# Local-global attention with a gated MLP: TensorE blocks of two attention units, scores four units ahead, residual halves added early, and the order drawn from 40 plans

## The chip, the cores and the metric

The kernel runs on one core of one Trainium2 chip. The metric is device microseconds (us) of one execution. The kernel before takes 427.39 us, the median of three runs (426.9 to 428.18).

## What is computed

Two stages follow each other for each of 4 batches. The first is attention with 8 heads, 768 positions and head size 64, in which a query sees the first 8 positions and the last 96, with a bias linear in the distance. The second is a gated MLP over the 768 x 512 result.

```python
scores = scale * q @ k^T + bias            # kept: key < n_global, or 0 <= rel < n_local
a = softmax(where(keep, scores, -1e9)); x = a @ v          # heads side by side: 768 x 512
h = gelu(x @ w_in); u, v = halves of h
v_n = (v - mean) / sqrt(var + 1e-6) * g_ln
v_s = w_sg @ v_n + b_sg                    # mixes the 768 positions
out = x + (u * v_s) @ w_out
```

## The kernel before, in words

**Attention** is cut into 48 units: a batch (4), two heads (4 pairs), and 256 query positions (3). Within a batch the four pairs of the first 256 positions come first. A unit has three pieces of TensorE work, all in 64x64 quarters of the array: the scores (`score`, matmuls on L714, into two PSUM banks), for the first 16 units a transposition by a diagonal matrix (`turn_quarters`, L845, two banks), and p.v (`weigh`, L873, two banks named av). p.v has a first part and a second, `again`, which adds into the same columns and so waits until the first part is done; between the two, TensorE has the scores of another unit. After the scores, VectorE adds the bias and takes the minimum (L745), ScalarE takes the exponential (L750), and for units from the 17th p is divided by its sum on GpSimd, ScalarE or VectorE (L767), transposed in 32x32 blocks by VectorE (L809) and sent through DRAM by DMA (far, then pt). The av banks are read out as two halves, x and the rest that x lost in rounding, by L929 and L933 from the 25th unit on (L947, L959, L961, L965 before).

**The MLP** runs in full 128x128 matmuls, three for each product (high x high, high x low, low x high: L413, L414, L415, called `terms`). Its tiles are v (512 columns; gelu and norm), u (384; gelu), mix (w_sg times the normed v, then times u) and out. An out tile adds both halves of x to the bank (L524 for the first, L526 for the second) and is sent off on SyncE's queue (L529).

**What sets the order.** The program is written down as a list of operations, each with the engines that may do it and a cost on each. `Plan.due` gives each operation a time at which it is needed. `Plan.order` then walks through time: on each free engine it starts the operation that is due first among those whose inputs are there and whose buffers have a place. TensorE's list is kept nearly in the written order. Numbers steer it: CALM and PATIENCE (an operation that is not urgent may wait for a cheaper engine), PRICE (a surcharge on VectorE), EARLY (how long ahead a load may be issued), SPARE (how many further PSUM banks must be free before an MLP tile opens one), TO_QUARTERS and FROM_QUARTERS (what TensorE loses when it goes from whole-array matmuls to quarters and back). What comes out is a fixed order on each engine's queue. Buffers have the places that PLACES gives: 8 PSUM banks, 2 each of v and pt, 4 of p, 3 of qk, 1 of tt, 4 of t.

**The written order** comes from `step(n)`: load v for n + 1 and qk for n + 4, first part of p.v of unit n, transposition of unit n + 1, scores of unit n + 3 (AHEAD is 3), second part of p.v of unit n, softmax of n + 3. `phase` puts MLP products between the steps. So TensorE goes into quarters once for each unit, for one block of p.v and scores, and back. In the last phase o[1][0..2], three out tiles, take turns product by product, and the fourth follows.

**At the start** VectorE makes the table of distances (L600, L601 and L655 to L667) from GpSimd's iota rows and from n_global and n_local, which come by DMA (tile ni). The bias of each head is made from it (L685, L687). TensorE is given matmuls on zeros (L364) where it would idle up to 29 us.

## Time and profile before

| | us |
|---|---|
| median of 3 runs | 427.39 |
| the profiled execution | 425.15 |
| its span, first to last instruction | 423.3 |
| TensorE (PE) busy | 407.6, 96% |
| VectorE (DVE) busy | 304.6, 72% |
| ScalarE (ACT) busy | 235.1, 56% |
| GpSimd (POOL) busy | 202.0, 48% |

A profile row gives the line of the kernel, the engine, the operation, the tile written and those read, the shapes and the count. In a timeline, the first two numbers are the start and the length in us. Matmuls overlap: the time that one really costs is from its start to the next one's start, not its length. An fp32 matmul in quarters shows as two records, so 4 matmuls in an order are 8 in a timeline.

### The profile page before, as it was taken

The numbers are of one execution on the slowest core, as the hardware profiler recorded it, in microseconds if no ns is written. First come the engines' busy times: TensorE is split into PE (matmuls) and PEld (weight loads), VectorE is DVE, ScalarE is ACT, GpSimd is POOL, SyncE is SP. The second block draws the span as 40 slices with busy tenths as digits, with TensorE's granted clock in tenths as the row PEclk, the third lists the DMA queues.
The fourth block names the chain that finished last, engine by engine and source line by source line (L and its number), as shares of the span: only waits on it lengthen the run. The fifth ranks groups of instructions, "written<-read, shape, count | busy, mean of one in ns | idle before, by whom it ended". The sixth has DMA issues, their size and how long they took to land.

```text
span 423.3 us, 13841 instructions
## 1 busy us (share of the span) xinstructions
PE 407.6 (96%) x5328; PEld 370.6 (88%) x5328; DVE 304.6 (72%) x990; ACT 235.1 (56%) x787; POOL 202.0 (48%) x312
## 2 busy tenths in 40 slices
PE   8989999899999999999999999999999999999994
PEld 8877777799888888999999888999999878999994
DVE  6887899999966879866566888966566866743343
ACT  5999989866657575654246566554245434311220
POOL 2223446668577586452545466452545443323211
PEclk9999999999999999999999999999999999999998
DMA  7656493347888776553877766463886631001002
GB/s 250 217 183 187 153 291 111 125 131 215 241 258 275 197 246 168 133 153 106 242 234 219 213 197 177 125 158 108 244 248 170 168 108 38 2 0 57 19 2 81
DMA packets 50041, 68.22 MB, mean 161 GB/s; under 512 B 5808, under 2 KB 33968, under 8 KB 49968
## 3 DMA queue, kind: packets, MB, share of 16 engines
q1 hardware_dynamic: 49968, 67.26, 54.2%
q8 instruction: 44, 0.72, 0.7%
q14 instruction: 29, 0.24, 0.2%
HBM read 48.89 MB, written 18.35 MB: 159 GB/s over the span
## 4 chain that ended last, share of the span: by engine, by line
PE 76%; DVE 9%; ACT 7%; DMA 3%; issue 2%; POOL 1%; SPq 0%; POOLq 0%; DVEq 0%
PE mm_ps L413 21%; PE mm_ps L415 19%; PE mm_ps L414 19%; PE av L873 8%; PE s_ps L714 6%; ACT p L750 3%; PE tps L845 2%; DMA far<-tt 2%; DMA stage<-in_w_sg_t_dram 1%; DVE stage L570 1%; DVE stage L572 1%; DMA ni<-in_n_gl_dram 1%; DVE p L745 1%; DVE o L524 1%; DVE tt L809 1%
## 5 line engine op out<-in xcount | busy, mean ns | idle before, releaser
L750 ACT ACTIVATE p<-p,pst 128x192 f32<-128x192 f32 x192 | 84.1, 443 | 7.4 <-DVE pst L745 6.9
L767 POOL TENSOR_SCALAR p<-p,pst 128x192 f32<-128x192 f32 (+1 forms) x128 | 56.0, 454 | 21.9 <-DVE pst L759 15.4
L413 PE MATMUL mm_ps<-wsg,z 128*128 128x384 f32 x192 | 65.1, 339 | 0.4 <-ACT pt L853 0.4
L415 PE MATMUL mm_ps<-wsg,z 128*128 128x384 f32 x192 | 64.3, 335 | 0.0
L745 DVE CUSTOM_DVE_ANT_0 p<-s_ps,bias 128x192 f32<-128x192 f32 x192 | 57.3, 340 | 9.7 <-PE s_ps L714 9.4
L414 PE MATMUL mm_ps<-wsg,z 128*128 128x384 f32 x192 | 64.3, 335 | 0.0
L873 PE MATMUL av<-pt,v 64*64 64x128 f32 (+1 forms) x1408 | 54.6, 254 | 2.6 <-DMA far<-tt 1.7
L873 PEld LDWEIGHTS av<-pt,v 64*64 64x64 f32 x1408 | 38.8, 133 | 16.8 <-issue 7.0
L526 POOL TENSOR_TENSOR o<-o,x 128x384 f32<-128x384 f32 x30 | 30.4, 1014 | 44.5 <-DVE o L524 31.9
L413 PE MATMUL mm_ps<-x,win 128*128 128x384 f32 x128 | 44.3, 346 | 0.8 <-ACT pt L853 0.8
L714 PE MATMUL s_ps<-qk 64*64 64x128 f32 (+1 forms) x1408 | 42.5, 247 | 1.7 <-issue 1.0
L413 PE MATMUL mm_ps<-gt,wout 128*128 128x384 f32 x128 | 43.0, 336 | 0.0
L415 PE MATMUL mm_ps<-gt,wout 128*128 128x384 f32 x128 | 43.0, 336 | 0.0
L415 PE MATMUL mm_ps<-x,win 128*128 128x384 f32 x128 | 42.9, 335 | 0.0
L414 PE MATMUL mm_ps<-x,win 128*128 128x384 f32 x128 | 42.8, 335 | 0.0
L414 PE MATMUL mm_ps<-gt,wout 128*128 128x384 f32 x128 | 42.8, 335 | 0.0
L506 POOL TENSOR_TENSOR y<-y,u 128x384 f32<-128x384 f32 x20 | 20.3, 1014 | 43.0 <-DVE y L503 28.2
L413 PE MATMUL mm_ps<-win,x 128*128 128x512 f32 x96 | 40.4, 421 | 0.0
L445 ACT CAST gt<-y 128x384 fp32r<-128x384 f32 x29 | 14.9, 512 | 45.9 <-DVE y L506 23.5
L714 PEld LDWEIGHTS s_ps<-qk 64*64 64x64 f32 x1408 | 37.5, 134 | 2.7 <-issue 1.3
L413 PEld LDWEIGHTS mm_ps<-wsg,z 128*128 128x128 f32 x192 | 36.0, 188 | 2.1 <-issue 1.4
L415 PE MATMUL mm_ps<-win,x 128*128 128x512 f32 x96 | 37.6, 392 | 0.0
(105 smaller groups left out, 937.7 us busy)
## 6 DMA issues: line engine op xcount, KB each, us to landing
qk<-in_qk_in_dram SPq DMA_DIRECT2D x32, 352.0 KB, 3.9
far<-tt SPq DMA_DIRECT2D x96, 96.0 KB, 2.6
pt<-far SPq DMA_DIRECT2D x24, 384.0 KB, 3.5
v<-in_v_in_dram SPq DMA_DIRECT2D x32, 256.0 KB, 3.3
out_dram<-o SPq DMA_DIRECT2D x32, 192.0 KB, 2.8
qk<-in_qk_in_dram SPq DMA_DIRECT2D x16, 288.0 KB, 3.6
v<-in_v_in_dram SPq DMA_DIRECT2D x16, 192.0 KB, 3.6
far<-tt SPq DMA_DIRECT2D x32, 80.0 KB, 1.9
```

Of the source, the lines that this page charges most:

```text
L413: mm(ps.ap, ah, bh, start=(i == 0), stop=False)
L414: mm(ps.ap, ah, bl, start=False, stop=False)
L415: mm(ps.ap, al, bh, start=False, stop=(i == n - 1))
L445: put(out[:, 0, :], src.ap)
L506: by_u = lambda eng: eng.tensor_tensor(y.ap, y.ap, gt.ap, ALU.mult)
L526: lo = lambda eng: eng.tensor_tensor(o.ap, o.ap, xm[:, 1, :].bitcast(F32), ALU.add)
L714: nc.tensor.matmul(s_ps[h][e * HQ:(e + 1) * HQ, i * W + c0:i * W + c0 + n], qk[rows, qc:qc + HQ], qk[rows, QW + k0:QW + k0 + n], start=Tru ...
L745: nc.vector.tensor_tensor_reduce(out=p[:, g, 0:nk], in0=s_ps[h][:, i * W:i * W + nk], in1=bias[:, 2 * j + h, w0:w0 + nk], op0=ALU.add, op1 ...
L750: op([on_act(nk, 0.225) + (lambda p=p, g=g, nk=nk, i=i: nc.scalar.activation(p[:, g, 0:nk], p[:, g, 0:nk], AF.Exp, bias=st[:, 0, i, g:g + ...
L767: op([on_pool_ts(nk, -0.10) + (partial(scaled, lambda o, a, c: nc.gpsimd.tensor_scalar(o, a, c, 1.0, ALU.mult, ALU.mult)),), on_act(nk, 0. ...
L845: nc.tensor.matmul(tps[r][g * HQ:(g + 1) * HQ, a * HQ:(a + 1) * HQ], pc[rows, c:c + HQ], diag[rows, 2 * i + c // W], start=True, stop=True)
L873: nc.tensor.matmul(to, v[rows, vc:vc + D], of, stop=True, skip_group_check=True, **kw)
```

## The change

From the 25th unit on (PAIRS = 24) `step` takes two units: it writes down the scores of one unit, the first parts of p.v of both, the scores of the next unit, then both second parts. The pair shares two av banks (columns 0 to 127 and 128 to 255). Scores are then written four units ahead of the pair instead of three. For out tiles of the last half of the last batch, the two halves of x are added to each other in advance (L548 of the new kernel, after the tile's first product), and one add of the bank follows. The distances take fewer VectorE operations, and those that don't need n_global and n_local come first. FROM_QUARTERS goes from 0.11 to 0.21, the spare banks from 2 to 0 once the scores of 27 units are written down. `order` draws CALM, EARLY, PRICE and a small shift of each due time from a seed; 40 seeds are planned and the plan that ends first by the planner's own clock is emitted.

```diff
-CALM, PATIENCE = 5.0, 2.0
-PRICE = 0.3
-EARLY = 12.0
+PLANS = 40
+CALM, PATIENCE = (3.0, 12.0), 2.0
+PRICE = (0.1, 0.4)
+EARLY = (9.0, 17.0)
+APART = 0.2
-SPARE = 2
+SPARE, SPARE_LATE = 2, 0
+PAIRS = 24
-TO_QUARTERS, FROM_QUARTERS = 0.095, 0.11
+TO_QUARTERS, FROM_QUARTERS = 0.095, 0.21
...
-        for o in self.order(start):
+        self.due()
+        ends = [self.order(start, seed)[1] for seed in range(PLANS)]
+        for o in self.order(start, ends.index(min(ends)))[0]:
...
+        whole = self.temp("o", CH) if last else None
+
+        def ahead(first):
+            xm = x[m][c]
+            both = lambda eng: eng.tensor_tensor(whole.ap, xm[:, 0, :].bitcast(F32),
+                                                 xm[:, 1, :].bitcast(F32), ALU.add)
+            op([on_dve_sb(CH) + (lambda: both(nc.vector),),
+                on_pool(CH) + (lambda: both(nc.gpsimd),)], [xm], [whole], [first])
...
-    future(rel, tmp)
...
+    def distances():
+        future(rel, tmp)
...
+        vec.tensor_scalar(key, key, ng, FAR, ALU.is_ge, ALU.mult)
+        vec.scalar_tensor_tensor(tmp, rel, nl, key, ALU.is_ge, ALU.mult)
+        vec.scalar_tensor_tensor(dist[:, 0:W], rel[:, 0:W], nl, tmp[:, 0:W], ALU.min, ALU.max)
+        vec.scalar_tensor_tensor(dist[:, 2 * W:], rel[:, W:], nl, tmp[:, W:], ALU.min, ALU.max)
...
-    dist_b.since = 6.3
+    dist_b.since = 5.6
...
         def put():
-            shared(0)
-            for e in range(2):
...
+            for m in range(len(ns)):
+                shared(m, 0)
+                for e in range(2):
...
-    def step(n):
-        m = n + AHEAD
...
+    def group(n):
+        return list(range(n, n + 1 + (n >= PAIRS)))
+
+    def step(ns):
+        nonlocal scored
+        end = ns[-1] + 1
+        nexts = [n for n in group(end) if 0 <= n < len(units)]
+        more = list(range(scored, min(end + AHEAD + (end >= PAIRS), len(units))))
+        scored += len(more)
...
+        for n in more[:-1]:
+            score(n, [])
+        if end > 0:
+            first, rest = weigh(ns)
+        for n in nexts:
+            turn(n)
+        for n in more[-1:]:
...
+            between.append(score(n, [first] if first else []))
```

**The blocks.** On TensorE, around the last phase of the third batch, a block of one unit before (p.v of the 36th unit, scores of the 39th):

```order
L415 MATMUL mm_ps<-gt,wout 128x384
L873 MATMUL av<-pt,v 64x128 x4
L873 MATMUL av<-pt,v 64x64 x8
L714 MATMUL s_ps<-qk 64x128 x8
L714 MATMUL s_ps<-qk 64x64 x4
L873 MATMUL av<-pt,v 64x128 x4
L413 MATMUL mm_ps<-win,x 128x512
```

After, the block with p.v of the 33rd and 34th unit (L761 are the scores, L922 is p.v):

```order
L435 MATMUL mm_ps<-wsg,z 128x384
L761 MATMUL s_ps<-qk 64x128 x8
L761 MATMUL s_ps<-qk 64x64 x4
L922 MATMUL av<-pt,v 64x128 x4
L922 MATMUL av<-pt,v 64x64 x8
L922 MATMUL av<-pt,v 64x128 x4
L922 MATMUL av<-pt,v 64x64 x8
L761 MATMUL s_ps<-qk 64x128 x8
L761 MATMUL s_ps<-qk 64x64 x4
L922 MATMUL av<-pt,v 64x128 x8
```

Two units' work now stands in one stretch of quarters. Counted over the whole order, from the first block of the 25th unit to the end there were 27 such stretches and are now 16: nine blocks of a pair in one piece, three pairs that the planner tore into two, and one block with the scores of the 29th unit alone. Up to there it was 23 stretches and is 23.

**The end.** On VectorE, the last rows of the program, before (gt and y belong to the last mix tile):

```order
L503 SCALAR_TENSOR_TENSOR y<-mm_ps,g,bsg 128x384
L506 TENSOR_TENSOR y<-y,u 128x384
L449 TENSOR_TENSOR gt<-y,gt 128x384
L524 TENSOR_TENSOR o<-mm_ps,x 128x384
L526 TENSOR_TENSOR o<-o,x 128x384
L524 TENSOR_TENSOR o<-mm_ps,x 128x384 x2
L526 TENSOR_TENSOR o<-o,x 128x384
L524 TENSOR_TENSOR o<-mm_ps,x 128x384
```

After, the sums of the halves of x (L548) stand between the last mix tile's operations and one add for each tile is left (L556); GpSimd's queue, which held the other two L526, holds none at the end:

```order
L525 SCALAR_TENSOR_TENSOR y<-mm_ps,g,bsg 128x384
L548 TENSOR_TENSOR o<-x 128x384
L528 TENSOR_TENSOR y<-y,u 128x384
L548 TENSOR_TENSOR o<-x 128x384 x2
L471 TENSOR_TENSOR gt<-y,gt 128x384
L556 TENSOR_TENSOR o<-mm_ps,o 128x384 x3
L548 TENSOR_TENSOR o<-x 128x384
L556 TENSOR_TENSOR o<-mm_ps,o 128x384
```

The four L548 are new on VectorE, and no add of x follows the last product but one.

**The start.** VectorE's rows for the distances after the change (L633 and L634 are the two of `future`, L703 is the first that needs ni; before, the two stood behind it, as L600 and L601):

```order
L633 TENSOR_SCALAR setup<-setup 128x320
L634 TENSOR_TENSOR setup<-setup 128x320
L703 SCALAR_TENSOR_TENSOR nv<-ni 128x2
L704 SCALAR_TENSOR_TENSOR nv<-nv,ni 128x2
L707 TENSOR_SCALAR setup<-setup,nv 128x320
L708 SCALAR_TENSOR_TENSOR setup<-setup,nv 128x320
L709 SCALAR_TENSOR_TENSOR dist<-setup,nv 128x192
L710 SCALAR_TENSOR_TENSOR dist<-setup,nv 128x128
```

Two rows moved ahead of the wait for ni, and two fewer follow it. Elsewhere operations went from one engine to another: of the halves of z, y and gt, 28 went from GpSimd to VectorE, and of L767, 22 went from GpSimd to ScalarE and 3 to VectorE.

## The prediction

> **What bounds the kernel now.** I read the page's first part, then busy time in windows, then TensorE's timeline at two blocks, then its waits, and last the two ends.

> ```profile
> PE 407.6 (96%) x5328; PEld 370.6 (88%) x5328; DVE 304.6 (72%) x990; ACT 235.1 (56%) x787; POOL 202.0 (48%) x312
> ```

> TensorE (PE) leads by far, but a busy PE isn't yet a PE that does work. Where it is short of work the windows say:

> ```profile
> core 0: us, PE busy (x) PEld busy (x) DVE busy (x) ACT busy (x) POOL busy (x), PEclk, DMA share, GB/s
> 20.00:31.00 11.00, 9.50 (x347) 8.23 (x347) 9.83 (x30) 10.37 (x40) 3.88 (x4) 1.00 0.64 207
> 31.00:40.00 9.00, 8.01 (x241) 6.47 (x238) 5.85 (x30) 8.20 (x32) 2.60 (x6) 1.00 0.65 186
> 60.00:90.00 30.00, 27.25 (x383) 24.14 (x383) 27.55 (x89) 26.02 (x87) 18.38 (x25) 1.00 0.40 121
> 120.00:130.00 10.00, 9.05 (x107) 8.39 (x106) 5.73 (x20) 4.74 (x20) 6.39 (x10) 1.00 0.96 307
> 130.00:153.00 23.00, 21.71 (x320) 18.88 (x319) 17.44 (x56) 13.29 (x49) 15.43 (x28) 1.00 0.81 233
> 165.00:260.00 95.00, 95.00 (x1126) 86.90 (x1122) 69.16 (x234) 51.04 (x172) 49.23 (x82) 1.00 0.66 185
> ```

> The column that matters is PE busy beside the length. Up to 31 us ScalarE (ACT) sets the pace, busy 10.37 of 11.00. Between 31 and 153 PE lacks 0.99, 2.75, 0.95 and 1.29 us in four windows, 6.0 together. From 165, where the 25th unit's block begins, it lacks nothing, at full clock (PEclk 1.00): there the time is what PE's instructions cost, and only fewer or cheaper ones shorten it. What a block of quarters costs beside its matmuls shows in the timeline, first where a block is whole, then where the same p.v is in two pieces:

> ```profile
> 207.50 0.34 PE L415 MATMUL mm_ps<-gt,wout 128*128 128x384 f32 x1
> 207.77 0.68 PE L873 MATMUL av<-pt,v 64*64 64x128 f32 x24
> 208.27 0.85 PE L714 MATMUL s_ps<-qk 64*64 64x128 f32 x32
> 208.94 0.40 PE L873 MATMUL av<-pt,v 64*64 64x128 f32 x8
> 209.27 0.44 PE L413 MATMUL mm_ps<-x,win 128*128 128x384 f32 x1
> 209.55 0.34 PE L414 MATMUL mm_ps<-x,win 128*128 128x384 f32 x1
> ```

> ```profile
> 334.30 0.33 PE L414 MATMUL mm_ps<-gt,wout 128*128 128x384 f32 x1
> 334.47 0.34 PE L415 MATMUL mm_ps<-gt,wout 128*128 128x384 f32 x1
> 334.74 0.68 PE L873 MATMUL av<-pt,v 64*64 64x128 f32 x24
> 335.35 0.50 PE L413 MATMUL mm_ps<-win,x 128*128 128x512 f32 x1
> 335.69 0.39 PE L414 MATMUL mm_ps<-win,x 128*128 128x512 f32 x1
> 335.92 0.40 PE L415 MATMUL mm_ps<-win,x 128*128 128x512 f32 x1
> 336.24 0.45 PE L873 MATMUL av<-pt,v 64*64 64x128 f32 x8
> 336.62 0.50 PE L413 MATMUL mm_ps<-win,x 128*128 128x512 f32 x1
> 336.96 0.39 PE L414 MATMUL mm_ps<-win,x 128*128 128x512 f32 x1
> ```

> From start to start a 384-column matmul takes 0.17 us (334.30 to 334.47), a 512-column one 0.23 (335.69 to 335.92). The whole block stretches the two steps from 207.50 to 209.55 to 2.05 us; less 2 x 0.17 it costs 1.71. Its scores run from 208.27 to 208.94, 0.67, so p.v with one entry and one exit costs 1.04. In two pieces the same p.v costs 1.22 - 0.17 - 0.23 = 0.82 (334.47 to 335.69) and 1.04 - 2 x 0.23 = 0.58 (335.92 to 336.96), 1.40 together. One more entry and exit therefore costs **0.36 us**.

> **The change part by part. Fewer blocks.** By the order, from the 25th unit on TensorE enters quarters 16 times instead of 27, with the same matmuls. 11 x 0.36 = 4.0 us, all of it in the stretch where PE lacks nothing, so it comes off the end if no wait takes its place. [...] The rows with p.v whole and in pieces measure the thing itself, so the sum goes by 0.36.

> **The end.** The last gt and the product that reads it, and then the last chain of work:

> ```profile
> 410.91 0.56 DVE L449 TENSOR_TENSOR gt<-y,gt 128x384 fp32r<-128x384 f32 x1 [0.58 <-ACT gt L445]
> 413.53 0.33 PE L413 MATMUL mm_ps<-gt,wout 128*128 128x384 f32 x1
> 417.00 0.34 PE L415 MATMUL mm_ps<-gt,wout 128*128 128x384 f32 x1
> 417.38 0.56 DVE L524 TENSOR_TENSOR o<-mm_ps,x 128x384 f32<-128x384 f32 x1
> 418.07 0.99 POOL L526 TENSOR_TENSOR o<-o,x 128x384 f32<-128x384 f32 x1 [1.03 <-DVE o L524]
> 415.50 3.92 SPq L529 DMA_DIRECT2D out_dram<-o  x4
> ```

> After, the store can go when L524's successor is done: 417.94 instead of 419.06, 1.1 us less; SyncE's queue, which issues the four stores up to 419.42, waits for nothing else then. The four sums of x halves stand on VectorE (DVE) instead, at about 0.56 us each by L524. Three stand in the last mix tile's chain: one delays its gt by 0.56, the other two fall into the 0.58 that DVE waited there and delay it by 2 x 0.56 - 0.58. gt was ready at 411.47 and is read from 413.53 on, so these 1.1 us stay hidden; without that cover they would cost 1.1, the whole gain. The fourth sum fits in DVE's wait for the last product. I take 1.1, with 0 as the other end.

> **The start.** The distances on VectorE, from the first row that needs ni to the first bias:

> ```profile
> 3.80 0.16 DVE L655 SCALAR_TENSOR_TENSOR nv<-ni 128x2 f32<-128x2 int32 x1 [2.81 <-DMA ni<-in_n_gl_dram]
> 4.48 0.32 DVE L601 TENSOR_TENSOR setup<-setup 128x320 bf16<-128x320 bf16 x1
> 4.84 0.30 DVE L660 TENSOR_SCALAR setup<-setup,nv 128x320 bf16<-128x320 bf16 x1
> 5.18 0.33 DVE L662 TENSOR_TENSOR setup<-setup 128x320 bf16<-128x320 bf16 x1
> 5.42 0.30 DVE L663 TENSOR_SCALAR setup<-setup,nv 128x320 bf16<-128x320 bf16 x1
> 6.37 0.29 DVE L685 TENSOR_SCALAR bias<-dist 128x512 bf16<-128x512 bf16 x1
> ```

> L600 and L601 move into the wait of 2.81 us, and L660 and L662 become one operation, as do L663 and the two L664, L665. From start to start L601 costs 0.36 us, L660 0.34 and L662 0.24; with L663 and L600 taken at 0.24 like the last, 1.2 us leave the chain. No row shows a fused operation; each of the three may take up to 0.12 more than what it replaces (0.36 against 0.24), so 0.8 to 1.2 are left, and I take 0.8. ACT, which paces the first 31 us, starts by as much sooner; its order there is nearly the same. Ends: 1.2, and 0 if a load becomes the later one.

> **The drawn plan.** In the first 24 units the order enters quarters 23 times as before, and MLP products lie about where they lay. So the 6.0 us that PE lacks between 31 and 153 can shrink or grow, and no row says which. I take 0, with 4.0 less (two thirds of it gone) and 5.0 more (nearly as much again) as ends.

> **The moved operations.** 28 operations of 0.56 to 0.69 us go from GpSimd (POOL) to DVE, about 17 us on an engine that is busy 69.16 of 95 us from 165 to 260. PE covers it; if DVE were late, a bank would come free late, which is the second rival. The guard of p.v (L899) now holds its engine's queue until both first parts are done, by the rows above some 0.5 us longer, once for two units; what stands behind it there is late by that, beside PE's next products.

> Sum: -4.0 - 1.1 - 0.8 = **-5.9 us**. The profiled execution has 425.15 (span 423.3 and 1.85 around it) and would come to 419.25. The median of before lies 2.24 above that execution, so I forecast 427.39 - 5.9 = **421.5 us**.

> **The rivals.** *Transfers of a pair come late (slower).* v and pt have two places each, and a pair holds all four until its block ends. Both units' transfers must then land before the next block:

> ```profile
> pt<-far SPq DMA_DIRECT2D x24, 384.0 KB, 3.5
> v<-in_v_in_dram SPq DMA_DIRECT2D x32, 256.0 KB, 3.3
> PE av L873 <- DMA far<-tt: 1.7, 2, 1.0
> ```

> That is 1280 KB, 4.2 us at the 307 GB/s of the busiest window, and a landing of 3.5: 7.7 us. The shortest stretch between whole pairs has 54 matmuls, 54 x 0.17 = 9.2 us. The margin of 1.5 us is gone if other loads of SyncE's queue stand in front. The waits row shows PE standing up to 1.0 us for such a transfer. At 1.0 us for each of 12 pairs the change loses 12 - 5.9 = 6.1: 433.5 us. It decides from 0.49 us a pair. Against it: from 165 to 260 PE waits for no transfer though the traffic per unit is the same, and scores lead p.v by more time than before. Chance 0.09.

> *Banks are emptied late (about no change).* A whole pair fills 6 of 8 banks at once, and no spare is kept.

> ```profile
> L745 DVE CUSTOM_DVE_ANT_0 p<-s_ps,bias 128x192 f32<-128x192 f32 x192 | 57.3, 340 | 9.7 <-PE s_ps L714 9.4 <-DVE bias L685 0.2
> L933 DVE TENSOR_TENSOR x<-av,x 128x128 fp32r<-128x128 f32 x48 | 12.0, 283 | 0.0
> ```

> To empty them takes DVE 8 x 0.34 + 4 x 0.28 = 3.8 us, while PE fills the other two banks in 2 x 12 x 0.17 = 4.1. With 0.9 us of other work in front of DVE, PE waits 0.6 after each of 9 pairs, 5.4: 427 us. [...] Against it: av comes free early, and DVE has 27% to spare. Chance 0.10.

> *The drawn plan also takes early waits:* 4.0 us more, 417.5. Chance 0.16. *The drawn plan is worse early on:* 5.0 us more, 426.5. Chance 0.08. That the change doesn't do what it says is out, as the order shows the pairs.

> **How the numbers follow.** The forecast has what is left, 0.57, with a range of its own from 419 to 424 (one of the two small terms missing, or 2 us of waits either way). 417.5 belongs to a case of 0.16, so the range begins at 416.5; upward it takes in the worse plan and the late banks and ends at 427, which leaves out the late transfers and a little of each other case. About 0.3%, 1.3 us, is what a measurement of this kernel can tell from no change. Faster: 0.57 + 0.16, and 0.07 of the bank and worse-plan cases, 0.80. Same: 0.07 of these. Slower: the late transfers and 0.04 of these, 0.13.

> **What would show it.** Right: in the profile after, a whole pair block of 1.71 + 1.71 - 0.36 = 3.06 us from product to product, PE full from the 25th unit on, the last store issued within 0.8 us of the last product's end, the first bias begun before 5.7 us. Wrong: rows of PE's waits with av behind a DMA, or products behind DVE, in the second half; or a first product of the MLP as late as before and larger gaps before 153.

## The result

The changed kernel takes 422.93 us, the median of 19 runs (421.12 to 426.99), against 426.54 for the kernel before in 19 runs beside it (424.92 to 429.69): a ratio of 0.9917, 95% interval 0.9892 to 0.9942. The forecast was 421.5, with 416.5 to 427.0 as its range and 0.80 for faster. The profiled execution of the changed kernel took 422.89, its span 421.1. A ratio here is not the quotient of the two medians (for e9 below that would be 0.9903, where the ratio is 0.9876); where the two tell clearly different sizes, both are given.

### The profile page after: what moved, and what is told of

Same layout as the page of the kernel before. It is cut to its first block, busy times and chain, and to the rows that moved or that the text cites. A ratio compares the mean times of both kernels' runs of the same rounds, so it can differ in the third digit from the quotient of the medians.

```text
span 421.1 us, 13845 instructions
## 1 busy us (share of the span) xinstructions
PE 403.9 (96%) x5334; PEld 371.2 (88%) x5334; DVE 317.9 (75%) x1022; ACT 242.5 (58%) x811; POOL 158.3 (38%) x254
## 4 chain that ended last, share of the span: by engine, by line
PE 66%; DVE 15%; DMA 6%; ACT 6%; issue 3%; SPq 2%; POOL 1%; DVEq 0%; POOLq 0%
PE mm_ps L433 18%; PE mm_ps L435 17%; PE mm_ps L434 17%; PE av L922 6%; PE s_ps L761 5%; ACT p L797 2%; DVE p L792 2%; DMA pt<-far 2%; DMA far<-tt 2%; PE tps L892 2%; SPq L864 2%; DVE stage L603 1%; DVE tt L856 1%; DVE stage L605 1%; DMA qk<-in_qk_in_dram 1%
## 5 line engine op out<-in xcount | busy, mean ns | idle before, releaser
L797 ACT ACTIVATE p<-p,pst 128x192 f32<-128x192 f32 (+1 forms) x192 | 84.2, 444 | 26.2 <-DVE pst L792 26.0
L814 POOL TENSOR_SCALAR p<-p,pst 128x192 f32<-128x192 f32 (+1 forms) x103 | 46.7, 470 | 70.0 <-DVE pst L806 52.1
L792 DVE CUSTOM_DVE_ANT_0 p<-s_ps,bias 128x192 f32<-128x192 f32 (+1 forms) x192 | 56.9, 338 | 7.1 <-PE s_ps L761 6.9
L922 PE MATMUL av<-pt,v 64*64 64x128 f32 (+1 forms) x1408 | 48.1, 251 | 4.9 <-DMA pt<-far 1.5
L922 PEld LDWEIGHTS av<-pt,v 64*64 64x64 f32 x1408 | 36.8, 134 | 13.9 <-issue 2.2
L559 POOL TENSOR_TENSOR o<-o,x 128x384 f32<-128x384 f32 x28 | 28.7, 1028 | 50.6 <-DVE o L556 33.1
L761 PE MATMUL s_ps<-qk 64*64 64x128 f32 (+1 forms) x1408 | 41.2, 249 | 0.4 <-DMA qk<-in_qk_in_dram 0.4
L761 PEld LDWEIGHTS s_ps<-qk 64*64 64x64 f32 x1408 | 36.2, 134 | 6.0 <-issue 4.3
L433 PE MATMUL mm_ps<-win,x 128*128 128x512 f32 x96 | 40.2, 419 | 0.0
L434 PE MATMUL mm_ps<-win,x 128*128 128x512 f32 x96 | 37.7, 393 | 0.0
L435 PE MATMUL mm_ps<-win,x 128*128 128x512 f32 x96 | 37.7, 392 | 0.0
## 6 DMA issues: line engine op xcount, KB each, us to landing
pt<-far SPq DMA_DIRECT2D x24, 384.0 KB, 4.4
v<-in_v_in_dram SPq DMA_DIRECT2D x32, 256.0 KB, 4.1
```

The lines of the kernel that those rows point to most:

```text
L433: mm(ps.ap, ah, bh, start=(i == 0), stop=False)
L434: mm(ps.ap, ah, bl, start=False, stop=False)
L435: mm(ps.ap, al, bh, start=False, stop=(i == n - 1))
L559: lo = lambda eng: eng.tensor_tensor(o.ap, o.ap, xm[:, 1, :].bitcast(F32), ALU.add)
L761: nc.tensor.matmul(s_ps[h][e * HQ:(e + 1) * HQ, i * W + c0:i * W + c0 + n], qk[rows, qc:qc + HQ], qk[rows, QW + k0:QW + k0 + n], start=Tru ...
L792: nc.vector.tensor_tensor_reduce(out=p[:, g, 0:nk], in0=s_ps[h][:, i * W:i * W + nk], in1=bias[:, 2 * j + h, w0:w0 + nk], op0=ALU.add, op1 ...
```

## The profile after

Where the forecast hung on single rows, here are the rows that answer. First the page's busy times, then the same windows as before (busy time of each engine in each stretch):

```profile
PE 403.9 (96%) x5334; PEld 371.2 (88%) x5334; DVE 317.9 (75%) x1022; ACT 242.5 (58%) x811; POOL 158.3 (38%) x254
```

```profile
20.00:31.00 11.00, 8.57 (x299) 7.56 (x300) 7.76 (x28) 8.37 (x32) 1.73 (x2) 1.00 0.61 196
31.00:40.00 9.00, 8.88 (x275) 7.09 (x265) 6.92 (x34) 8.34 (x33) 3.65 (x7) 1.00 0.70 195
60.00:90.00 30.00, 28.32 (x459) 24.35 (x451) 29.28 (x101) 27.26 (x92) 14.23 (x17) 1.00 0.41 125
120.00:130.00 10.00, 9.81 (x151) 8.75 (x142) 6.23 (x19) 5.72 (x19) 3.57 (x7) 1.00 0.84 256
130.00:153.00 23.00, 22.57 (x303) 19.74 (x303) 18.79 (x65) 17.93 (x64) 9.36 (x15) 1.00 0.78 220
165.00:260.00 95.00, 94.93 (x1121) 88.57 (x1120) 74.83 (x246) 52.91 (x185) 40.50 (x74) 1.00 0.69 198
```

From 165 to 260 PE is as full as before, so no wait took the place of the blocks that went. From 20 to 31 it lacked 1.50 us before and now lacks 2.43. In the four windows between 31 and 153 that lacked 6.0 us together it now lacks 2.4, so in this profile the plan took early waits out, 3.6 us of the 4.0 that the forecast gave to that rival. It is one profile: from 31 to 160 PE lacks 5.0 us in it, 7.0 in the second one of the same kernel (e12 below) and 6.0 in the kernel before. A whole block of two units on PE, in the timeline:

```profile
209.92 0.34 PE L435 MATMUL mm_ps<-gt,wout 128*128 128x384 f32 x1
210.19 0.90 PE L761 MATMUL s_ps<-qk 64*64 64x128 f32 x32
210.91 1.08 PE L922 MATMUL av<-pt,v 64*64 64x128 f32 x48
211.81 0.85 PE L761 MATMUL s_ps<-qk 64*64 64x128 f32 x32
212.48 0.62 PE L922 MATMUL av<-pt,v 64*64 64x128 f32 x16
213.03 0.44 PE L433 MATMUL mm_ps<-x,win 128*128 128x384 f32 x1
213.31 0.33 PE L434 MATMUL mm_ps<-x,win 128*128 128x384 f32 x1
```

From 209.92 to 213.31 are 3.39 us; less 2 x 0.17 for the two products the block costs 3.05, where 3.06 was forecast. Worked out in this way from all records, the 27 stretches of quarters from the 25th unit on cost 39.4 us before and the 16 after 35.1. Those before hold 24 records of scores more, which the changed kernel has ahead of its first pair; at 0.67 us for 32 that is 0.5, so 3.8 went. PE's busy time tells the same without any choice of stretches: 407.6 us on the page before, 403.9 after, **3.7 us** less for the same matmuls (forecast 4.0).

The end, in the timeline of SyncE's queue, PE and VectorE:

```profile
413.04 3.46 SPq L562 DMA_DIRECT2D out_dram<-o  x4
415.20 0.34 PE L435 MATMUL mm_ps<-gt,wout 128*128 128x384 f32 x1
415.58 0.56 DVE L556 TENSOR_TENSOR o<-mm_ps,o 128x384 f32<-128x384 f32 x1 [1.06 <-PE mm_ps L435]
```

One add follows the last product, and the queue is through at 416.50, 0.96 us behind the product's end (415.54); before it was 419.42 against 417.34, 2.08. The last store's issue begins at 416.17, 0.63 behind the product, within the 0.8 that was forecast. So the chain is 1.1 us shorter, as forecast. The span does not end 1.1 sooner, though: from the last product's start to the last instruction 5.91 us pass, 6.28 before.

The start, VectorE's timeline:

```profile
3.91 0.16 DVE L703 SCALAR_TENSOR_TENSOR nv<-ni 128x2 f32<-128x2 int32 x1 [0.73 <-DMA ni<-in_n_gl_dram]
4.38 0.30 DVE L707 TENSOR_SCALAR setup<-setup,nv 128x320 bf16<-128x320 bf16 x1
4.72 0.55 DVE L708 SCALAR_TENSOR_TENSOR setup<-setup,nv 128x320 bf16<-128x320 bf16 x1
5.31 0.42 DVE L709 SCALAR_TENSOR_TENSOR dist<-setup,nv 128x192 bf16<-128x192 bf16 x1
5.64 0.35 DVE L710 SCALAR_TENSOR_TENSOR dist<-setup,nv 128x128 bf16<-128x128 bf16 x1
6.21 0.29 DVE L732 TENSOR_SCALAR bias<-dist 128x512 bf16<-128x512 bf16 x1
```

The first bias begins at 6.21 instead of 6.37, not before 5.7. The first row that needs ni starts 0.11 later than before, and the fused rows take 0.55 us for 320 elements and 0.42 for 192, where the unfused ones took 0.30 to 0.33 for 320. From its start to the next one's L708 costs 0.59 us, where the forecast allowed a fused row 0.36. PE's waits over the whole span, the two largest rows (total, times, longest):

```profile
PE tps L892 <- issue: 2.4, 2, 2.1
PE av L922 <- DMA pt<-far: 1.5, 2, 1.1
```

The longest, 2.1 us, is one in which PE waited for nothing that the profile shows; it lies at 24.66, ahead of the first MLP product, which starts at 33.53 instead of 31.01. The span of the profiled executions can be added up. Up to the start of its last product PE is busy 403.6 us, 407.2 before, and idle 11.7 us, 9.8 before; the end is 0.4 shorter: -3.7, +1.9 and -0.4 are the 2.2 us between 423.3 and 421.1. What of the idle time is the draw's doing no row of one profile can say. That needed kernels that take the change apart.

## The experiments

The first theory was A: the blocks and the end bring what was forecast, and the draw took some of it back ahead of the 31st us. The kernel before takes 425.26 us beside the first four kernels. "Undrawn" means one plan with the numbers of the kernel before:

```diff
-PLANS = 40
-CALM, PATIENCE = (3.0, 12.0), 2.0
-PRICE = (0.1, 0.4)
-EARLY = (9.0, 17.0)
-APART = 0.2
+PLANS = 1
+CALM, PATIENCE = (5.0, 5.0), 2.0
+PRICE = (0.3, 0.3)
+EARLY = (12.0, 12.0)
+APART = 0.0
```

**The change without the draw (e1).** This edit alone.

> All of the change but the draw: the planner's numbers are fixed at those of before (5.0, 0.3, 12.0, no shift), one plan. Theory A (the drawn plan gives time back before 65 us, the rest of the change brings what its parts say): blocks -4.0 us, end -1.1, start -0.2, so about 5 us under before, a ratio of 0.988, and a first MLP product before 31.5 us against 33.5 in the changed kernel. Rival B (the draw is neutral, the blocks or the end bring less than they seem): the ratio of the whole change, 0.992, and a first product near 33.

425.21 us, ratio 0.9988 (0.9954 to 1.0022). Theory A falls: without the draw the rest of the change brings nothing that can be measured, and the draw is worth 3.0 us (0.9917 against 0.9988), or 2.3 by the changed kernel's second measurement (e12, 0.9933), whose interval overlaps this one. In the profile, which is of the longest of its 12 executions (429.19 us), the first pair shows what the forecast's first rival described, at this one place (timeline of PE, then windows with the granted clock behind POOL's column):

```profile
174.48 0.67 PE L922 MATMUL av<-pt,v 64*64 64x128 f32 x16
177.90 0.50 PE L922 MATMUL av<-pt,v 64*64 64x128 f32 x10 [2.75 <-DMA pt<-far]
```

```profile
174.30:178.70 4.40, 1.65 (x53) 1.34 (x55) 4.22 (x15) 2.40 (x10) 2.46 (x5) 1.00 0.30 84
178.70:182.10 3.40, 3.40 (x46) 2.78 (x39) 2.21 (x8) 2.06 (x8) 2.60 (x5) 0.51 0.83 199
```

The second unit of the pair waits 2.75 us for its transposed p, and then PE runs at half its clock (0.51) for 3.4 us. How many of the shorter executions, from 422.24 us, have this wait too is not shown.

**Without the pairs as well (e2).** `PAIRS = 99` and undrawn: start, end and the planner's new price.

> As e1, but no pairs: each unit has its own block of quarters again. Theory A: the pairs' 4.0 us are missing, so 4 us over e1, a ratio to before of about 0.997. Rival B: the pairs are worth 2.5 us or less, so e2 stands 2.5 us or less over e1.

427.2 us, ratio 1.0057 (1.0031 to 1.0082): slower than the kernel before. So something in the start, the end or the price costs, and the pairs are worth 0.0069 of 425 beside it, 2.9 us (2.0 by the medians). `PAIRS = 99` also keeps the spare banks at two, since the kernel lowers them only behind `PAIRS + AHEAD` units; so the pairs are measured together with that edit, here and below.

**With the old start (e3).** Undrawn, with pairs, end and new price, but the distances as before:

```diff
-    in_turn(distances)
+    nc.vector.tensor_scalar(tmp, rel, nl, FAR, ALU.is_ge, ALU.mult)
...
-    dist_b.since = 5.6
+    dist_b.since = 6.3
```

> As e1, but the distances are made as before, with the two operations of future behind the wait and nothing fused. By the trace of the changed kernel (first bias at 6.21 us against 6.37) the start is worth 0.2 us: no difference to e1 that can be measured. By the forecast's step it is worth 0.8 us: 0.8 us over e1, its first product 0.8 us later.

425.93 us, ratio 1.0027 (0.9997 to 1.0057); the first pair waits 2.6 us here too, again in the longest of 12 executions. The new start is not what costs, as long as the new price is there. The old start has a second number in it, the time at which the planner takes SyncE's queue to be free (1.0 us, 0.7 in the changed kernel); e4, e9 and e10 go back to it too.

**The kernel before with the draw alone (e4).** The drawn numbers and the 40 plans of the changed kernel, put into the kernel before, and nothing else.

> The kernel before with nothing but the draw: 40 plans, the shortest by the planner's clock. Theory A: the drawn plan costs 1 to 2 us, a ratio of 1.003 to 1.005, lost before 100 us. Rival B: no difference, 0.998 to 1.002. If the draw does what it is for: under 0.997.

424.81 us, ratio 0.9984 (0.9951 to 1.0017). The draw by itself brings nothing sure. It pays only beside the other edits.

That suggested theory U: the other edits upset the single order that the planner's rule falls into, and the draw finds a better one. It can be read from the planner itself. By its own clock, the waits of TensorE behind the first MLP product are 6.2 us in the kernel before and 10.4 in each of the three undrawn kernels above; in the drawn plan of the changed kernel they are 4.6. Whether that clock says anything of the chip was theory D, tested with two other draws, one for each direction, beside two more kernels (the kernel before: 425.55).

**The worst of the forty draws (e5).**

```diff
-        for o in self.order(start, ends.index(min(ends)))[0]:
+        for o in self.order(start, 2)[0]:
```

> The changed kernel with the draw that its planner liked least of the forty: the planner's clock ends at 420.74 us instead of 411.66. Theory D, the planner's clock is a fair forecast of the chip: from the kernel without draws (planner 416.35, ratio to the kernel before 0.9988) to the one with them (411.66, 0.9917) the chip gave 3.0 us for 4.7 us of the planner's, or 0.65 us for each; so 9.08 us later by the planner is 5.9 us later on the chip, some 428.8 us, ratio about 1.0055, with the loss in waits of TensorE, not in the blocks of quarters. Rival L, the draw that was taken was lucky on the chip and the planner's clock does not rank the orders: any draw lands near 0.995, this one too. Rival W, the draw's whole gain was that the first pair of units did not wait for its transfer: this one is at 0.9917 or 0.9988, according to whether its first pair waits under 0.5 us or about 3 us.

427.92 us, ratio 1.0050 (1.0024 to 1.0076), where theory D said 1.0055. The planner's list has 13.7 us of waits behind the first MLP product, half of it one wait of 7.55 at a product; the chip shows a wait there too, and the halved clock behind it:

```profile
PE mm_ps L433 <- ACT wsg L608: 2.3, 1, 2.3
```

```profile
77.40:81.60 4.20, 1.70 (x9) 1.38 (x9) 4.06 (x14) 0.91 (x3) 1.23 (x2) 1.00 0.34 109
81.60:88.50 6.90, 6.06 (x17) 4.90 (x18) 6.87 (x21) 3.71 (x9) 0.74 (x1) 0.51 0.44 144
```

The product waits for w_sg, which ScalarE turns into high and low parts too late. Rival W falls: this order's first pair waits 0.4 us, and the loss lies elsewhere.

**The best of 1640 draws (e6).** The same edit with 665 in place of 2.

> The changed kernel with the best of 1640 draws instead of the best of 40: the planner's clock ends at 410.29 us instead of 411.66. Theory D: 1.37 us at 0.65 is 0.9 us less, ratio about 0.9896. Rival L: no rank, anything between 0.990 and 0.999, the middle at 0.995. By either the steady blocks of two units stay at 3.04 us.

421.84 us, ratio 0.9914 (0.9877 to 0.9952). Theory D said 0.9896, inside the interval, and so is the drawn kernel's 0.9917: a gain of 1.37 us by the planner's clock is too small to be seen. Rival L, by which every draw would land near 0.995, is out by the worst draw.

**Wider fillers (e7).** The matmuls on zeros that keep PE busy up to 29 us write the whole bank at once, in the changed kernel's own order:

```diff
-        for _ in range(int((gap - 1.0) / 0.108 if first else (gap - 0.25) / 0.06)):
-            self.tc.nc.tensor.matmul(to[:, 0:P], self.on, self.on, start=True, stop=True)
+        n = int((gap - 1.0) / 0.108 if first else (gap - 0.25) / 0.06)
+        k = min(to.ap.shape[1], FF) // P
+        for cols in [k * P] * (n // k) + [P] * (n % k):
+            self.tc.nc.tensor.matmul(to[:, 0:cols], self.on[:, 0:P], self.on[:, 0:cols],
+                                     start=True, stop=True)
```

> The changed kernel in its own order, with the filler products of the first 31 us as wide as the bank that they write (256 to 512 columns) instead of 128, and so many fewer: about 100 products and their weight loads less. Theory I, the 2.1 us in which TensorE waited for nothing that the profile shows (24.66 to 26.76) is the fetch of its next 256 instructions, which arrives 1.5 us after its packet landed at 25.29: with fewer instructions the fetches come later and further apart there, the wait falls under 1.0 us, the first MLP product starts at 31.5 to 32.5 instead of 33.4, and the time falls by 1 to 1.5 us, ratio 0.988 to 0.9895. Rival: the wait belongs to a signal that the profile does not show: it stays at 2 us at the same product, first MLP product at 33.4, ratio 0.9917.

427.29 us, ratio 1.0004 (0.9968 to 1.0039): 3.7 us slower than the changed kernel by the ratios, and the expected gain did not come. The longest wait now lies at 14.05 instead of 24.66, and the clock was halved behind it (timeline of PE, then a window with the clock):

```profile
13.44 0.61 PE L764 MATMUL s_ps<-qk 64*64 64x128 f32 x12
16.17 0.69 PE L764 MATMUL s_ps<-qk 64*64 64x128 f32 x8 [2.12 <-issue]
```

```profile
15.80:22.60 6.80, 6.43 (x127) 5.83 (x126) 4.05 (x15) 4.26 (x16) 1.23 (x2) 0.50 0.28 86
```

Three more such waits of 0.59 to 1.23 us follow before 60, and the first MLP product starts at 37.55. Where the theory of instruction fetches stands is told below, under the hardware.

**Undrawn with the old price (e8).** FROM_QUARTERS back to 0.11, pairs, end and new start kept.

> The change without the draw (as e1), and with the planner's price for leaving quarters put back from 0.21 to 0.11 us. Theory P, the new price alone made the planner's single order worse (waits before 160 us 10.8 us in e1 against 8.57 in the kernel before): they fall to about 8.6 and the ratio from 0.9988 to about 0.994. Rival, the price changes little and it is the pairs that upset an order laid out without draws: the first pair waits about 3 us again and the ratio stays at 0.9988.

425.89 us, ratio 0.9995 (0.9964 to 1.0026). Theory P falls: the price alone isn't it. But neither is its rival right: the first pair doesn't wait here. So the loss lies ahead of it. The last four kernels were made for that (the kernel before: 425.27 beside them).

**Pairs and end only (e9).** Old start and old price, undrawn: the two diffs above and `FROM_QUARTERS = 0.11`.

> Only the blocks of two units from the 25th unit on and the last x halves added under the products; start, planner's prices and single order as before. Theory U: what e1 lacked was lost because the new start and the new price upset the planner's one order ahead of the 153rd us (its own clock counts 10.4 us of TensorE's waits behind the first MLP product in e1, 6.2 in the kernel before, 5.6 here), while the blocks of two and the end give what their rows say: 3.7 us of blocks and 0.4 to 1.1 us at the end, some 422 us, ratio about 0.990, waits of TensorE ahead of 160 us no more than the 8.6 us of the kernel before. Rival V, the blocks of two themselves upset the order without draws: the first pair waits about 3 us as in e1 and e3, ratio 0.997 to 1.000.

421.14 us, ratio 0.9876 (0.9839 to 0.9914), where theory U said 0.990. Theory U also said that PE would wait no more ahead of 160 us than in the kernel before, and that missed: counting all its idle time, PE is idle 11.9 us up to there, 9.8 before. The first pair doesn't wait, and PE is full:

```profile
165.00:260.00 95.00, 95.00 (x1123) 88.79 (x1122) 69.38 (x240) 51.63 (x183) 50.69 (x86) 1.00 0.70 200
```

Rival V falls. This is also the fastest kernel of the study: 1.65 us under the changed kernel's 422.79 beside it, though the two intervals (0.9839 to 0.9914 and 0.9900 to 0.9967) overlap a little, and in the two kernels' profiles (422.60 and 422.89 us) the last product starts at the same 415.20.

**Pairs only (e10).** The same without the sums of halves at the end (`last` is False).

> e9 without the end: only the blocks of two units. Theory U: ratio 0.991 to 0.993; against e9 it is later by the end's worth, 1.1 us (0.0026) if the forecast's term stands, 0.4 to 0.7 us (0.0010 to 0.0016) if the profiles of the changed kernel and of the kernel before tell it rightly, whose time from the last product to the end of the span is 6.0 and 6.4 us. Rival V: 0.998 to 1.001.

421.31 us, ratio 0.9894 (0.9849 to 0.9940): the pairs are worth 4.5 us, 2.6 to 6.4 (4.0 by the medians), which holds both the forecast's 4.0 and the rows' 3.7. PE's busy time up to the start of its last product, before and then in e10, shows where they come from:

```profile
0.00:417.00 417.00, 407.23 (x5327) 370.60 (x5328) 303.70 (x989) 235.13 (x787) 200.97 (x311) 1.00 0.55 162
0.00:414.25 414.25, 403.19 (x5328) 371.07 (x5328) 300.92 (x987) 233.84 (x788) 199.39 (x312) 1.00 0.55 163
```

PE is busy 4.0 us less for the same matmuls, both at full clock. The end's 0.0018 is within the intervals; it is left to the profiles.

**The start only (e11).** The distances in fused rows, `PAIRS = 99`, no early halves, old price, undrawn.

> Only the distances in fused rows at the start, with the planner's clock for them 0.7 us earlier, single order. Theory U: the planner's one order is upset by this alone: its clock ends at 418.96 us against 413.79 of the kernel before, with 13.3 us of waits against 6.2 behind the first MLP product; at 0.65 to 1 us of the chip for each us of the planner that is 3.4 to 5.2 us slower, ratio 1.008 to 1.012, the waits of TensorE ahead of 160 us above 12 us. Rival, the forecast's own term: the start is worth 0.2 to 0.8 us and the rest of the order is as good as before, ratio 0.998 to 1.000.

427.8 us, ratio 1.0057 (1.0027 to 1.0086): 2.4 us slower, as theory U said in sign, somewhat less than its 3.4 to 5.2. Its waits ahead of 160 us are not above 12 as expected: PE is idle 9.6 us up to there, no more than the 9.8 of the kernel before. What the new order waits for, the two largest waits of PE between 60 and 130 us show, first here, then in e8, which has the same start, then in e9, which has the old one:

```profile
PE tps L892 <- POOL diag L824: 2.7, 2, 2.5
PE mm_ps L435 <- POOL wout L610: 1.3, 1, 1.3
```

```profile
PE tps L892 <- POOL diag L824: 2.4, 1, 2.4
PE mm_ps L435 <- POOL wout L610: 1.3, 1, 1.3
```

```profile
PE mm_ps L433 <- ACT pt L897: 1.3, 2, 0.8
PE tps L889 <- issue: 0.7, 1, 0.7
```

With the new start and the old price the planner has GpSimd make a diagonal and split w_out too late, both at the same places on the chip, and neither in the old order. By the planner's own clock the diagonal's wait is 2.04 us, at 69.98. A start that is 0.7 us sooner on paper thus gives an order that is 2.4 us worse. That these two waits are the whole loss is not shown, for other waits went with the old order. Up to its last product PE is idle 9.6 us in e11, 9.8 before; what is longer is its busy time, 409.4 us against 407.2. Of these 2.2 us the clock can account for 1.8, as an estimate: the wait for the diagonal ends at 72.70, and the mean granted clock from 60 to 90 us is 0.94. In e8's profile it is 1.00 from 60 to 90, and PE's busy time is 2.5 us longer than in e9 all the same (405.7 against 403.3); why is open. In the planner it is the start's time alone that upsets the order: its clock ends at 418.96 with 5.6 for 6.3, and at 413.79 as before with SyncE's 0.7 for 1.0.

**The changed kernel once more (e12)**, unaltered.

> The changed kernel once more, unaltered, for its second profile. Theory I, TensorE's waits on nothing that the profile shows are fetches of instructions, which end at fixed counts of products (221, 348, 474, 601, 727, 980, 1233, 1360 and 1486 in nine kernels of different orders, 126.5 apart): the wait comes back at the 601st product, which resumes 1.3 to 1.6 us behind the landing of a 16 KB packet, though its length may differ, as the packet's start does. Rival, an accident of one execution: no wait there. The ratio is again 0.989 to 0.994.

422.79 us, ratio 0.9933 (0.9900 to 0.9967), an interval that holds the first measurement's 0.9917. The wait at the 601st matmul is there again, 1.67 us long, so it is no accident.

All kernels together; planner's waits are those behind the first MLP product by the planner's own clock, the granted clock is the median of a kernel's executions, and the other times come from the profiles:

| kernel | planner's waits | first MLP product | first block with p.v of the 25th unit | last product | ratio | granted clock |
|---|---|---|---|---|---|---|
| before | 6.2 | 31.01 | 164.38 | 417.00 | 1 | 0.997 |
| e4 before, drawn | 4.5 | 31.63 | 166.7 | 416.53 | 0.9984 | 0.9935 |
| e11 start only | 13.3 | 30.68 | 166.4 | 419.06 | 1.0057 | 0.9925 |
| e2 no pairs | 10.4 | 30.68 | 166.6 | 419.55 | 1.0057 | 0.995 |
| e10 pairs only | 5.6 | 30.60 | 171.93 | 414.25 | 0.9894 | 0.997 |
| e9 pairs and end | 5.6 | 32.08 | 172.88 | 415.20 | 0.9876 | 0.9985 |
| changed | 4.6 | 33.53 | 171.88 | 415.20 | 0.9917 | 0.996 |
| e7 wide fillers | 4.6 | 37.55 | 176.0 | 420.51 | 1.0004 | 0.992 |
| e6 best of 1640 | 3.0 | 34.50 | 170.78 | 413.40 | 0.9914 | 0.996 |
| e8 undrawn, old price | 12.7 | 31.09 | 174.50 | 416.82 | 0.9995 | 0.995 |
| e1 undrawn | 10.4 | 33.55 | 174.48 | 422.04 | 0.9988 | 0.992 |
| e3 undrawn, old start | 10.4 | 31.19 | 173.6 | 421.05 | 1.0027 | 0.992 |
| e5 worst of forty | 13.7 | 31.59 | 171.30 | 419.45 | 1.0050 | 0.990 |

But for e7, whose fillers the planner doesn't know, the kernels with pairs fall into two groups: up to 5.6 us of planned waits 0.988 to 0.993, over 10 us 0.999 to 1.005. Within a group the intervals allow no ranking. The granted clock goes with the groups: 0.9945 to 0.9985 in the first (0.9945 is e12), 0.990 to 0.995 in the second. As an estimate, what is missing to 1 times the kernel's time is clock that was not granted: 0.6 to 2.3 us in the first group, 2.1 to 4.3 in the second, 1.3 in the kernel before, where 1.1 of it costs nothing: in its profile the clock is 1.00 up to 417.4 and 0.51 from 421.0 to the end, behind the last product. Between the groups it differs by 1.8 us on average, of the 4.6 that lie between them; the rest is not taken apart. The four undrawn kernels with pairs and end make a square: old start and old price 0.9876, new start alone 0.9995, new price alone 1.0027, both 0.9988. Either of the two edits suffices to lose what pairs and end bring, and the draw wins half of it or more back (0.0055 to 0.0071 of 0.0112). Why the planner's rule falls into the worse order was not followed further.

## Why the prediction came out right, step by step

The direction and the time came out, on a sum in which one term of four was wrong in sign and another was put at nothing. That the time lies so near is luck in part: the loss by start and price was not in the forecast, nor that the draw would win back half of it or more, and the kernel before itself came out 0.85 us lower than the 427.39 that the sum begins from.

**Fewer blocks: right, 3.7 to 4.5 us for 4.0.** One entry and exit less saves what the rows of the whole and the torn block gave, 0.36 us (3.7 / 11 = 0.34 by PE's busy time in the changed kernel, 4.0 / 11 = 0.37 in e10).

**The end: mechanism right, size too large.** The store goes 1.1 us sooner after the last product, as the step said. But the last product to the last instruction takes 5.92 us on average in the ten profiles with the early halves (5.36 to 6.61) and 6.31 in the four without (6.27 to 6.36): 0.4 is left of 1.1, and two of the ten lie above 6.31. What takes the rest lies behind the last store's issue: from there to its landing 2.4 to 2.5 us pass in the four profiles without the early halves, and 2.2 to 3.9 in the ten with them, 3.1 on average. The step ended its chain at the issue and so took the landing to be the same. Why it takes longer is open.

**The start: wrong in sign.** The step gave 0.8 us and went by its chain alone. The fused rows ate the chain's gain (0.16 left; L708 alone took 0.59 us, where 0.36 was allowed), and the term left out that the planner reads the start's time: told of a start 0.7 us sooner, it wrote another order, 2.4 us slower on the chip.

**The drawn plan: not zero, but a repair.** The step took the draw at nothing against the order of the kernel before. Against the order that the other edits made, it is worth 2.3 to 3.0 us, which paid for half or more of what the start and the price had lost (e1 against e9: 0.0112, 4.8 us, or 4.1 by the medians). The price was no term of the sum at all. The rivals on the draw were put as its own deviation from the kernel before; the real one came from the planner's inputs.

**The sum.** In its second measurement the changed kernel was 2.5 us under the kernel before (422.79 against 425.27), in the first 3.6. By parts: blocks -3.7, end -0.4, and start, price and draw together +1.65 (by the medians against e9, which has none of them; the intervals of the two overlap a little), -2.45 in all. Of the forecast's 5.9, 0.3 failed in the blocks, 0.7 at the end and 0.8 + 1.65 in the start and the plan. The forecast named a late first product of the MLP together with larger gaps before 153 us as a sign of being wrong. Only the first half came: the product is 2.5 us later than before and 1.45 later than in e9, but the gaps in the four windows fell from 6.0 to 2.4 us, and the changed kernel's block of the 25th unit is 1.0 sooner than e9's.

**The rivals.** Late transfers showed at one pair of two undrawn kernels, at 2.6 to 2.75 us, and nowhere in the changed one beyond 0.29 us there. Late banks did not show in the second half of the changed kernel: VectorE, busy 74.83 of 95 us from 165 to 260, kept up, and the moved operations cost nothing there. Ahead of it they may have cost something: between 31 and 160 us 4.1 of the 5.0 us that PE waits stand behind VectorE's rows, 2.3 of 7.0 in e12, and none of 6.0 in the kernel before.

## What to carry to other kernels

Where a planner or a scheduler reads a number, an edit of that number is an edit of the whole order: cost it by what the new order waits for, not by the operation that the number describes. Undo each such edit alone before the sum is trusted: here either of two lost about 1%, and a search over orders hid half of it or more. A wait can cost more than its length, where the clock is halved behind it (in e1 3.4 us at 0.51 behind a wait of 2.75). Work inside a stretch where the leading engine lacks nothing can be costed to a tenth from the same work whole and in pieces (here 0.36 us for one entry and exit, against 0.34 and 0.37 by PE's busy time).

## What the runs showed of the hardware

```profile
24.23 0.34 PE L364 MATMUL av<-bsg 128*128 128x128 bf16 x3
25.41 0.38 PE L364 MATMUL av<-bsg 128*128 128x128 bf16 x4 [0.83 <-issue]
```

```profile
24.66 0.34 PE L381 MATMUL av<-bsg 128*128 128x128 bf16 x3
26.65 0.49 PE L381 MATMUL av<-bsg 128*128 128x128 bf16 x6 [1.66 <-issue]
```

In the changed kernel the packet lies at 24.48 to 25.42 and PE goes on at 26.76; the DMA view from 24.4 to 25.5 has it (packets, MB, share of the DMA engines):

```profile
q8 instruction: 1, 0.02, 5.3%
```

From one such matmul to the next packet's start 1.0 to 4.6 us pass up to 60 us, then 0.9 to 1.4 for the packet and about 1.4 more. Between 17 and 31 us 126 matmuls of the changed kernel take 3.7 to 4.3 us without that wait, fillers included, so the way over the packet was sometimes the longer one: in the changed kernel 5.8 us, from the 474th matmul at 20.96 to the 26.76. In e7, with 49 fewer fillers and as many weight loads less, the waits stayed at the same counts and so fell on other places: that speaks for the packets as what PE waited for, though the cure failed. What sets a packet's start was not shown.

**Behind some waits of about 2 us the clock was halved.** Waits of 1.76 (e4 at 55.7), 2.12 (e7), 2.3 (e5, e12), 2.4 and 2.6 (e3), 2.5 (e11) and 2.75 us (e1) were each followed by 3.4 or 6.8 us at a granted clock of 0.5; others of 2.10 (changed), 2.18 (e2), 2.28 (e1) and 2.38 us (e8) were not. The windows have 0.51 behind the wait in e1 and e5 and 0.50 in e7, and 1.00 from 20 to 40 us in the changed kernel and from 60 to 90 in e8. In the windows ahead of those three drops PE was busy 1.65 of 4.40 us (e1), 1.70 of 4.20 (e5) and 1.92 of 3.80 (e7). The length of the wait alone doesn't tell the two cases apart; what does was not shown.

**The fused rows in bf16 took longer on VectorE.** In the changed kernel a SCALAR_TENSOR_TENSOR took 0.35, 0.42 and 0.55 us for 128, 192 and 320 elements, 1.0 ns for each further element, while in the kernel before a TENSOR_SCALAR took 0.30 for 320 and a TENSOR_TENSOR 0.33. From start to start the fused L708 costs 0.59 us, and the L660 and L662 that it replaces cost 0.34 and 0.24: fusing the two brought nothing.
